# A long convolution with a routed expert layer: the matrices of the way back are turned on TensorE instead of loaded

## The chip, the cores and the metric

One core of a Trainium2 chip runs the whole program. The metric is the time of one execution in device microseconds (us). The engines are TensorE (PE in the rows, its weight loads PEld), VectorE (DVE), ScalarE (ACT), GpSimd (POOL) and SyncE (SP), which here only issues transfers. A row that ends in q (SPq, ACTq) is that engine's queue of instructions.

## The reference

Two layers follow each other. The first multiplies x and v (4 batches, 10048 positions, 128 channels), convolves the product over the positions with a filter that a small network makes, and multiplies by x again. The second sends every one of the 40192 rows to one of 16 experts and weighs what the expert gives.

```python
# first layer
h_filt = (np.maximum(pos_emb @ w1, 0.0) @ w2) * window
u = x * v
Uf = np.fft.rfft(u, n=2 * S, axis=1)
Hf = np.fft.rfft(h_filt, n=2 * S, axis=0)
y = np.fft.irfft(Uf * Hf[None, :, :], n=2 * S, axis=1)[:, :S, :]
x = (x * y).reshape(B * S, D)
# second layer: g = argmax(x @ w_group), e = argmax(x @ w_expert[g])
out = g_w * e_w * (np.maximum(x @ w1[g, e], 0.0) @ w2[g, e])
```

## The kernel before, in words

**The transform.** There is no FFT. A position is written as block times 128 plus place within the block, and the transform is done in two products with matrices of cosines and sines: one over the 79 blocks (`dft_blocks`, line 409), one over the 128 places within a block (`dft_positions`, line 487). Between them all of a batch lies in the tiles z and zr as frequency by channel: 128 places, 128 channels, 79 frequencies k, and two parts. All data are float32.

**Stages.** The filter goes first (up to about 143 us): its own transform ends in the DRAM array hspec. Then a loop runs over the batches b = 0 to 3 and once more for what is left of the last. For each batch:

- `dft_blocks` transforms the channels, three at a time, into z and zr. In the same loop the batch before comes out of z and zr: `turned` (lines 682 to 687) turns tiles through TensorE, ScalarE copies them to tiles tt, and `inverse_rest` and `inverse_blocks` (lines 697 and 718) make the second half of the inverse transform.
- Then 40 steps of `middle` and `back`, two frequencies each (the last has one). `middle` loads the filter's part ht (line 639). In every second step it loads four matrices bt from the constant c_b (line 644) and four matrices bp from the constant c_bp (line 645), one for each frequency: bt has the places on its partitions and the frequency's 128 outputs in its columns, and bp is the same matrix turned. `dft_positions` multiplies by bt into PSUM (tag ps, two buffers), VectorE multiplies by ht twice (lines 650 and 653), GpSimd adds and subtracts into y (lines 651 and 654). `back` is called LAG = 4 steps later: line 663 multiplies y by bp into PSUM (tag pt, four buffers), and ScalarE copies the result into z and zr (line 670), over what was read.
- While the steps of batch b run, the batch before it is routed, in pieces between the steps: `chosen` stores rows to DRAM (line 797), turns tiles of 128 by 128 through TensorE (line 800, copied by ScalarE at line 802), and multiplies them by the router's weights (lines 808, 817, 825). These turns, too, use PSUM's tag pt. `ranked` gives every row its place (VectorE, lines 854 to 894). Rows of batches ranked before are sent to the pages of their experts by GpSimd's indirect transfers (line 376), one in three steps of four.

Then the experts' pages are worked off (lines 1285 to 1376), from about 930 us on.

**What sets the order.** The transfers of lines 459 (input of the next batch), 639, 644, 645, 365 and 797 all stand in SP's queue. A transfer into a tile waits until the tile's buffer is free, and all behind it in the queue wait as well. bt shares five buffers (tag load) with the input xv; bp shares five (tag tt) with the turned tiles tt; ht shares five (tag spec) with the tiles xo. The order of each engine's instructions is fixed when the program is built, by a scheduler with a cost model that takes instructions by their place in the program as soon as it thinks them ready; some, such as the scatters, are held in the order in which the program names them. On the chip each engine takes its instructions in that order and stands where an operand is late.

A float32 matmul appears in the trace as two records of line 487 or 663; a turn as one.

Of the kernel before, what the change touches and what calls it, by code (L numbers as in the profile page):

```python
# [12 lines left out]
F32 = mybir.dt.float32  # L13
# [64 lines left out]
def make_consts():  # L78
    f32 = np.float32
    k1 = np.arange(NB)  # L80
    ang = 2 * np.pi * ((k1[None, :] * k1[:, None]) % N1) / N1
    w = (np.where(k1 == 0, 1.0, 2.0) / NN)[:, None]


    fa = np.stack(
        [
            np.stack([np.cos(ang), -np.sin(ang)], 2).reshape(NB, -1),
            np.stack([-np.sin(ang), -np.cos(ang)], 2).reshape(NB, -1),
        ],
        1,  # L90
    ).reshape(NB, -1)


    fi = []
    for swap in range(2):
        both = np.zeros((KM + 16, 2, NB))
        both[:NB, swap] = w * np.cos(ang)
        both[:NB, 1 - swap] = (2 * swap - 1) * w * np.sin(ang)
        rest = np.zeros((4, 32, 2, NB))
        for i in range(4):  # L100
            rest[i, :, i % 2] = both[KM:].reshape(32, NB)
        sign = 1 - 2 * swap
        fi += [sign * both[:KM].reshape(128, -1), sign * rest.reshape(128, -1)]
    fi = np.concatenate(fi, 1)
    k = k1[:, None] + N1 * np.arange(128)[None, :]
    s2 = 2 * np.arange(64) + 1
    a = np.pi * ((k[None] * s2[:, None, None]) % (2 * NN)) / NN
    b = np.concatenate([np.cos(a), np.sin(a)], 0)
    ph = (np.pi * ((k * 127) % (2 * NN)) / NN).T
    phase = np.stack([np.cos(ph), np.sin(ph), -np.cos(ph)], -1)  # L110
    win = np.zeros(NR * 128, f32)
    win[:SEQ] = np.exp(-0.01 * np.arange(SEQ, dtype=f32))
    win = win.reshape(NR, 128)
    return {
        "c_fa": np.concatenate([fa, np.zeros((NR - NB, 4 * NB))]),
        "c_fi": fi,
        "c_b": b,
        "c_bp": np.ascontiguousarray(b.transpose(2, 1, 0)),
        "c_phase": phase.reshape(128, NB * 3),
        "c_win": np.repeat(np.stack([win[:, 64:], win[:, 63::-1]]).transpose(0, 2, 1).reshape(2, -1), 64, 0),  # L120
        "c_tri": np.triu(np.ones((128, 128)), 1),
        "c_id": (np.arange(128)[:, None] * NB + np.arange(NB)[None, :]).astype(f32),
    }
# [26 lines left out]
class Kernel:  # L150
# [483 lines left out]
    def middle(self, b, k0, n):  # L634


        nc, d, sp = self.nc, self.d, self.sp
        ht = sp.tile([128, 2, 2, 128], F32, tag="spec", name="ht", bufs=NSPEC)
        nc.sync.dma_start(ht[:, :n], d["hspec"][:, k0 : k0 + n])
        if k0 % 4 == 0:  # L640
            self.bt = self.ap.tile([128, 4, 128], F32, tag="load", name="bt", bufs=NLOAD)
            self.bp = sp.tile([128, 4, 128], F32, tag="tt", name="bp", bufs=NTT)
            m = min(4, NB - k0)
            nc.sync.dma_start(self.bt[:, :m], d["c_b"][:, k0 : k0 + m])
            nc.sync.dma_start(self.bp[:, :m], d["c_bp"][:, k0 : k0 + m])
        bt, bp = self.bt[:, k0 % 4 :], self.bp[:, k0 % 4 :]
        ps = self.dft_positions(k0, n, bt)
        y = self.ap.tile([128, 2, 2, 128], F32, tag="y", name="y", bufs=NY)
        t0 = self.ap.tile([128, 2, 2, 128], F32, tag="prod", name="t0", bufs=NPROD)
        nc.vector.tensor_tensor(t0[:, :n], ps[:, :n], ht[:, :n], ALU.mult)  # L650
        nc.gpsimd.tensor_tensor(y[:, :n, 0], t0[:, :n, 0], t0[:, :n, 1], ALU.add)  # L651
        t1 = self.ap.tile([128, 2, 2, 128], F32, tag="prod", name="t1", bufs=NPROD)
        nc.vector.tensor_tensor(t1[:, :n], ps[:, :n], ht[:, :n, ::-1], ALU.mult)  # L653
        self.beyond(nc.gpsimd.tensor_tensor(y[:, :n, 1], t1[:, :n, 1], t1[:, :n, 0], ALU.subtract))  # L654
        return k0, n, bp, y
# [733 lines left out]
def build(nbat):  # L1389
    import concourse.bacc as bacc  # L1390

    nc = bacc.Bacc("TRN2", target_bir_lowering=False, num_devices=1, dynamic_dma_scratch_size=8192)
    shapes = {
        "xv_in": (nbat, NR, D, 2, 128),
        "x_out": (nbat, 128, D * NB),
        "pos_t": (128, 64 * NR),
        "p_w1": (128, 128),
        "p_w2": (128, 256),
        "w_router": (128, 32),
        "m_w1": (128, NE, FF),  # L1400
        "m_w2": (128, NE, FF),
        "c_iota": (128, 8 + NZ + 5 * NE),
    }
    for n, a in make_consts().items():
        shapes[n] = a.shape
    d = {n: nc.dram_tensor(n, s, F32, kind="ExternalInput").ap() for n, s in shapes.items()}
    d["out"] = nc.dram_tensor("out", (nbat * 128 * NB, D), F32, kind="ExternalOutput").ap()
    d["prow"] = nc.dram_tensor("prow", (Pages(nbat).rows, RW), F32, kind="Internal").ap()
    d["xyd"] = nc.dram_tensor("xyd", (nbat * 128 * NB, D), F32, kind="Internal").ap()
    d["hspec"] = nc.dram_tensor("hspec", (128, NB, 2, 128), F32, kind="Internal").ap()  # L1410
    with tile.TileContext(nc) as tc:
        Kernel(tc, d, nbat).emit()
    return nc


def layout(x, v, pos_emb, w1, w2, moe_w_group, moe_w_expert, moe_w1, moe_w2):
# [64 lines left out]
    for n, a in make_consts().items():  # L1481
        m[n] = c(a.astype(np.float32))
# [18 lines left out]
```

## Time and profile before

| | |
|---|---|
| median of three runs | 1888.68 us (1883.96 to 1894.56) |
| the profiled execution | 1889.78 us; span 1888.0 us |
| TensorE, weight loads | 1807.3 us (96%), 1522.5 us (81%) |
| VectorE, ScalarE, GpSimd | 1401.1, 1251.4, 1016.1 us (74%, 66%, 54%) |
| DMA | 343.81 MB, mean 182 GB/s |
| mean granted clock of TensorE | 0.989 of 2.4 GHz |

The profiled execution's own time holds some 1.8 us around the span, from the first to the last instruction. Busy time is the sum of an engine's instructions. Matmuls are pipelined: each has some 0.2 to 0.4 us from start to modelled end, and the next starts before that end, so the busy time of TensorE is not a measure of its room; the distance of two starts is. In the views used below, a line of the timeline merges neighbouring instructions of one kind (start, time from the first start to the last end, engine, line, tiles, count), and square brackets hold the idle time before it and what ended that. A wait for several things is put down to the one that came last.

### The profile page before, as it was taken

What the parts mean: (1) busy time and instruction counts of PE and PEld (TensorE: products, weight loads), DVE (VectorE), ACT (ScalarE), POOL (GpSimd) and SP (SyncE); (2) the same over time, 40 slices, a digit from 0 to 9 for tenths busy, and PEclk for the clock granted to TensorE, in tenths of its full rate; (3) what the DMA queues carried; (4) which work ended last, traced back from release to release, by engine and by line L of the source; (5) the groups of instructions that cost most, each with busy time, mean ns of one, the idle gap of its engine ahead of it and who ended that gap; (6) DMA issues with size and microseconds to landing.
All of it is one profiled execution on the core that took longest, in us unless ns stands there. A gap on an engine that the chain in (4) does not pass through costs nothing.

```text
span 1888.0 us, 43089 instructions
## 1 busy us (share of the span) xinstructions
PE 1807.3 (96%) x13958; PEld 1522.5 (81%) x13958; DVE 1401.1 (74%) x3140; ACT 1251.4 (66%) x2814; POOL 1016.1 (54%) x1172
## 2 busy tenths in 40 slices
PE   8988999999999999988899999999999999999998
PEld 7966888778877777767688888888888888889997
DVE  5577778689868975872879877777777777777886
ACT  6563368436743674456677777777777777777886
POOL 3236720464799478967245556666576333333354
PEclk9999999999999999999899999999999999999999
DMA  4599987987999799965563333444343223222342
GB/s 149 171 284 231 314 228 208 307 268 221 289 337 301 189 269 328 307 197 181 197 204 113 113 113 121 158 134 135 122 135 113 90 89 90 90 86 84 101 125 90
DMA packets 225451, 343.81 MB, mean 182 GB/s; under 512 B 28520, under 2 KB 110653, under 8 KB 225216
## 3 DMA queue, kind: packets, MB, share of 16 engines
q1 hardware_dynamic: 194208, 280.60, 49.3%
q0 software_dynamic: 21504, 44.82, 7.0%
q10 hardware_dynamic: 9504, 15.54, 3.0%
q8 instruction: 113, 1.85, 0.4%
q14 instruction: 122, 1.00, 0.2%
HBM read 265.88 MB, written 75.53 MB: 181 GB/s over the span
## 4 chain that ended last, share of the span: by engine, by line
PE 72%; DVE 9%; DMA 8%; issue 2%; ACT 2%; POOL 1%; SPq 1%; ACTq 0%; DVEq 0%; POOLq 0%
PE py L1352 8%; PE py L1350 8%; PE ph L1330 8%; PE ph L1332 8%; PE py L1351 8%; PE ph L1331 8%; PE psb L487 5%; PE pbp L663 4%; PE psa L409 3%; DMA xv<-xv_in 3%; PE po L718 2%; PE ptm L1364 2%; PE po L697 2%; PE px L1285 2%; DMA v<-xv_in 2%
## 5 line engine op out<-in xcount | busy, mean ns | idle before, releaser
L1339 DVE SCALAR_TENSOR_TENSOR hl<-ph,hh 128x512 fp32r<-128x512 f32 (+1 forms) x656 | 441.8, 674 | 157.5 <-ACT hh L1338 153.2
L1376 POOL DMA_INDIRECT out<-os,to x320 | 319.1, 997 | 416.4 <-ACT os L1371 344.0
L1338 ACT ACTIVATE hh<-ph 128x512 fp32r<-128x512 f32 (+1 forms) x656 | 388.7, 592 | 169.2 <-PE ph L1332 141.5
L376 POOL DMA_INDIRECT prow<-stg,adr x316 | 328.5, 1040 | 133.8 <-issue 61.8
L1330 PE MATMUL ph<-xh,wh 128*128 128x512 f32 (+2 forms) x720 | 280.9, 390 | 5.1 <-ACT wh L1312 5.1
L1332 PE MATMUL ph<-xh,wl 128*128 128x512 f32 (+2 forms) x720 | 265.8, 369 | 0.8 <-DVE ep L1247 0.8
L1331 PE MATMUL ph<-xl,wh 128*128 128x512 f32 (+2 forms) x720 | 264.7, 368 | 0.0
L1352 PE MATMUL py<-hh,wl 128*128 128x512 f32 (+2 forms) x720 | 264.6, 367 | 0.0
L1350 PE MATMUL py<-hh,wh 128*128 128x512 f32 (+2 forms) x720 | 264.5, 367 | 0.0
L1351 PE MATMUL py<-hl,wh 128*128 128x512 f32 (+2 forms) x720 | 263.3, 366 | 0.0
L670 ACT COPY z<-pbp 128x512 f32<-128x512 f32 x128 | 75.0, 586 | 179.3 <-PE pbp L663 173.8
L651 POOL TENSOR_TENSOR y<-t 128x256 f32<-128x256 f32 (+1 forms) x160 | 121.1, 757 | 132.0 <-DVE t L650 128.9
L409 PE MATMUL psa<-fa,eo 96*64 96x158 f32 x2048 | 171.4, 305 | 11.6 <-POOL eo L476 8.1
L487 PE MATMUL psb<-z,bt 128*128 128x256 f32 x640 | 162.7, 382 | 14.4 <-DVE t L653 5.8
L663 PE MATMUL pbp<-y,bp 128*128 128x256 f32 x632 | 162.8, 379 | 6.1 <-POOL y L654 4.2
L650 DVE TENSOR_TENSOR t<-psb,ht 128x512 f32<-128x512 f32 (+1 forms) x160 | 108.7, 679 | 73.6 <-POOL y L651 19.3
L409 PEld LDWEIGHTS psa<-fa,eo 96*64 96x64 f32 x2048 | 137.0, 139 | 28.2 <-POOL eo L476 12.7
L1332 PEld LDWEIGHTS ph<-xh,wl 128*128 128x128 f32 x720 | 136.7, 190 | 23.1 <-DVE ep L1247 1.1
L1330 PEld LDWEIGHTS ph<-xh,wh 128*128 128x128 f32 x720 | 137.2, 191 | 21.2 <-ACT wh L1312 5.6
L1351 PEld LDWEIGHTS py<-hl,wh 128*128 128x128 f32 x720 | 135.9, 189 | 21.9
L1352 PEld LDWEIGHTS py<-hh,wl 128*128 128x128 f32 x720 | 135.8, 189 | 21.9
L1350 PEld LDWEIGHTS py<-hh,wh 128*128 128x128 f32 x720 | 135.8, 189 | 21.3
(229 smaller groups left out, 3572.4 us busy)
## 6 DMA issues: line engine op xcount, KB each, us to landing
ws<-m_w SPq DMA_DIRECT2D x180, 256.0 KB
ht<-hspec SPq DMA_DIRECT2D x156, 256.0 KB
xv<-xv_in SPq DMA_DIRECT2D x131, 288.0 KB
bt<-c_b SPq DMA_DIRECT2D x95, 256.0 KB
bp<-c_bp SPq DMA_DIRECT2D x76, 256.0 KB
xyd<-xy SPq DMA_DIRECT2D x76, 256.0 KB
stg<-xyd SPq DMA_DIRECT2D x76, 256.0 KB
xg<-prow SPq DMA_DIRECT2D x66, 260.0 KB
```

Source lines behind the costliest of these rows:

```text
L376: ins = self.nc.gpsimd.indirect_dma_start(self.d["prow"], bass.IndirectOffsetOnAxis(ap=u.adr[:, t : t + 1], axis=0), u.rows[:, t - u.t0], ...
L409: ins = nc.tensor.matmul(ps[hs, i], eo[:, i, hs], self.fa[:, h], start=True, stop=True)
L487: nc.tensor.matmul(ps[:, i].rearrange("p s d -> p d s"), bt[:, i], self.frequency(k0 + i, 1)[:, :, 0], start=True, stop=True,)
L1330: k.fix(nc.tensor.matmul(ph[:, j], wh, self.xh, start=True, stop=False))
L1331: k.fix(nc.tensor.matmul(ph[:, j], wh, self.xl, start=False, stop=False))
L1332: k.fix(nc.tensor.matmul(ph[:, j], wl, self.xh, start=False, stop=True))
L1338: k.fix(nc.scalar.activation(hh, ph, AF.Relu))
L1339: k.fix(nc.vector.scalar_tensor_tensor(hl, ph, 0.0, hh.bitcast(F32), ALU.max, ALU.subtract))
L1350: k.fix(nc.tensor.matmul(self.py, wh, hh, start=(c == 0), stop=False))
L1351: k.fix(nc.tensor.matmul(self.py, wh, hl, start=False, stop=False))
L1352: k.fix(nc.tensor.matmul(self.py, wl, hh, start=False, stop=(c == NC - 1)))
L1376: ins = k.nc.gpsimd.indirect_dma_start(k.d["out"], bass.IndirectOffsetOnAxis(ap=self.to[:, h : h + 1], axis=0), o, None, bounds_check=k.nt ...
```

## The change

The constant c_bp and its load are gone. Where `middle` loads a group of bt, it takes a PSUM buffer of tag pt, turns each of the group's matrices (four, in the last group three) through TensorE against the identity, and lets ScalarE copy the whole group into bp. The tile bp stays where it was, with tag tt and five buffers.

```diff
@@ make_consts
         "c_b": b,
-        "c_bp": np.ascontiguousarray(b.transpose(2, 1, 0)),
         "c_phase": phase.reshape(128, NB * 3),
@@ middle
             self.bp = sp.tile([128, 4, 128], F32, tag="tt", name="bp", bufs=NTT)
             m = min(4, NB - k0)
             nc.sync.dma_start(self.bt[:, :m], d["c_b"][:, k0 : k0 + m])
-            nc.sync.dma_start(self.bp[:, :m], d["c_bp"][:, k0 : k0 + m])
+            pt = self.psT.tile([128, 4, 128], F32, tag="pt", name="ptb")
+            for i in range(m):
+                nc.tensor.transpose(pt[:, i], self.bt[:, i], self.ident)
+            nc.scalar.copy(self.bp[:, :m], pt[:, :m])
         bt, bp = self.bt[:, k0 % 4 :], self.bp[:, k0 % 4 :]
```

## Rows read from the trace of the kernel before

**Rows 1.** The chain that ended last, from the page of the whole execution.
```profile
PE 72%; DVE 9%; DMA 8%; issue 2%; ACT 2%; POOL 1%; SPq 1%; ACTq 0%; DVEq 0%; POOLq 0%
```

**Rows 2.** Instructions on tile bp: times (x) ns min/median/max, first and last start us.
```profile
L663 PE MATMUL pbp<-y,bp x632: 376/377/483, 182.8 to 822.8; 128*128 128x256 f32 x158
L645 SPq DMA_DIRECT2D bp<-c_bp x80: 327/382/1506, 171.7 to 803.3; - x80
```

**Rows 3.** Busy time of each engine in the windows M0, M1, M2 and M3.
```profile
core 0: us, PE busy (x) PEld busy (x) DVE busy (x) ACT busy (x) POOL busy (x), PEclk, DMA share, GB/s
...
179.20:252.00 72.80, 70.20 (x319) 59.00 (x320) 53.41 (x87) 23.02 (x41) 57.92 (x84) 1.00 0.91 288
...
336.00:432.50 96.50, 92.53 (x589) 71.65 (x585) 75.68 (x159) 40.78 (x96) 62.71 (x83) 1.00 0.87 285
...
521.00:624.00 103.00, 94.09 (x593) 71.37 (x589) 79.59 (x160) 40.87 (x97) 94.17 (x119) 1.00 0.91 302
...
721.00:823.50 102.50, 93.21 (x585) 71.42 (x579) 80.46 (x162) 40.55 (x95) 91.77 (x117) 1.00 0.84 282
```

**Rows 4.** Timeline of TensorE's weight loads, a step of M1 without routing.
```profile
410.66 0.84 PEld L487 LDWEIGHTS psb<-z,bt 128*128 128x128 f32 x4
411.53 0.83 PEld L663 LDWEIGHTS pbp<-y,bp 128*128 128x128 f32 x4
412.39 0.84 PEld L487 LDWEIGHTS psb<-zr,bt 128*128 128x128 f32 x4
```

**Rows 5.** Timeline of TensorE, a step of M1 with routing.
```profile
377.04 0.14 PEld L825 LDWEIGHTS pl<-ident,lt 128*128 128x128 f32 x1 [0.20 <-issue]
...
378.73 0.58 PEld L800 LDWEIGHTS ptr<-ident,xy 128*128 128x128 f32 x4
...
378.94 0.60 PE L800 MATMUL ptr<-ident,xy 128*128 128x128 f32 x4
...
379.83 0.14 PEld L825 LDWEIGHTS pl<-ident,lt 128*128 128x128 f32 x1 [0.20 <-ACT z L670]
```

**Rows 6.** Groups of instructions of the whole execution, shapes kept apart: busy us, mean ns.
```profile
L376 POOL DMA_INDIRECT prow<-stg,adr x316 | 328.5, 1040 | 133.8 <-issue 61.8 <-ACT zr L422 29.7 <-DMA xv<-xv_in 17.6
...
L651 POOL TENSOR_TENSOR y<-t 128x256 f32<-128x256 f32 x156 | 119.2, 764 | 131.9 <-DVE t L650 128.9 <-DVE c L870 0.8
...
L650 DVE TENSOR_TENSOR t<-psb,ht 128x512 f32<-128x512 f32 x156 | 107.1, 686 | 73.1 <-POOL y L651 19.3 <-POOL y L654 15.5 <-PE psb L487 13.2
...
L800 PE MATMUL ptr<-ident,xy 128*128 128x128 f32 x316 | 48.0, 277 | 4.0 <-DVE xy L735 4.0
...
L802 ACT COPY xrt<-ptr 128x512 f32<-128x512 f32 x76 | 44.3, 587 | 15.6 <-PE ptr L800 15.2
```

**Rows 7.** Timeline of TensorE's weight loads at the end of M2.
```profile
598.71 0.73 PEld L487 LDWEIGHTS psb<-zr,bt 128*128 128x128 f32 x4 [0.75 <-PE pbp L663]
...
605.84 0.73 PEld L487 LDWEIGHTS psb<-zr,bt 128*128 128x128 f32 x4 [1.05 <-PE pbp L663]
```

**Rows 8.** Waits of the whole execution: us in total, times, longest us.
```profile
DVE t L650 <- DMA ht<-hspec: 10.4, 5, 3.2
```

**Rows 9.** Timeline of M0: a load of bt, and TensorE's line 487 behind it.
```profile
184.76 0.38 SPq L644 DMA_DIRECT2D bt<-c_b  x1
...
189.01 1.97 PE L487 MATMUL psb<-z,bt 128*128 128x256 f32 x8 [0.40 <-DMA bt<-c_b]
...
199.69 1.11 PE L487 MATMUL psb<-z,bt 128*128 128x256 f32 x4 [1.03 <-DMA bt<-c_b]
```

**Rows 10.** Timeline of TensorE at the start of M1.
```profile
342.11 0.33 PE L825 MATMUL pl<-ident,lt 128*128 128x128 f32 x1
...
342.28 1.91 PE L487 MATMUL psb<-z,bt 128*128 128x256 f32 x8
...
347.28 1.11 PE L487 MATMUL psb<-z,bt 128*128 128x256 f32 x4 [0.75 <-DVE t L653]
```

## Prediction, made before the changed kernel was seen

> **What bounds the kernel now.** I read the page's chain first: TensorE fills 72% of the work that ended last, DMA 8% [rows 1]. That is an average over stages, so I asked which stages the change touches. The removed load is line 645's: 80 issues between 171.7 and 803.3 us [rows 2]. Cut by the first and last times of lines 487 and 663, there are four stretches of `middle` and `back`, one for each batch, called M0 to M3 here: 72.8, 96.5, 103.0 and 102.5 us, 374.8 in all [rows 3].
>
> In these stretches two rows of TensorE disagree. In M1 the matmuls are busy 92.53 of 96.50 us, the weight loads only 71.65 [rows 3]. The page says that ends of matmuls are modelled, so I went to starts. In a step of M1 without routing the four weight loads of line 487 start at 410.66, the four of line 663 at 411.53, and the next step's at 412.39: 1.73 us a step, each load beginning 0.03 us after the one before has ended [rows 4]. That is 1.73/8 = 0.216 us for each matmul. A batch has 158 records of line 663 (632/4, [rows 2]) and as many of line 487: 316 x 0.216 = 68.3 us, 94% of M0, where TensorE does nothing else. In M1 to M3 the routing of the batch before adds transposes and small matmuls: two such steps start their line 825 at 377.04 and 379.83, 2.79 us apart [rows 5]. The other engines need less for a step: two VectorE products of 0.69 us, two GpSimd sums of 0.76, a ScalarE copy of 0.59 or so [rows 6]. So TensorE sets the pace of M0, M1 and most of M2 and M3.
>
> The exception is the end of M2 and M3. From 598.71 to 605.84 us three steps of M2 take 2.38 us each, though TensorE still has 1.73 us of work; the weight loads wait 0.75 us before a step [rows 7]. GpSimd sets the pace there: two sums and, in three steps of four, a scatter of 1.04 us [rows 6] make 1.53 + 0.78 = 2.3 us.
>
> **The change, part by part.** Each time is of the profiled execution: span 1888.0, its own time 1889.78; the median of the runs is 1888.68, 1.1 less.
>
> *Removed: 80 loads*, some 20 MB, and 0.38 us of SP's queue for each [rows 2]. SP waits for buffers anyway, so the 0.38 us alone buy nothing. What the bytes can buy is what now ends in a wait on a transfer. VectorE waits 10.4 us for ht, five times [rows 8]. TensorE waits for bt twice, in M0: 0.40 us at 189.01, for a bt issued at 184.76, and 1.03 us at 199.69 [rows 9]. DMA is 0.91 busy there, at 288 GB/s [rows 3]; one bp less in front of each ht and bt brings these in. I take back the 1.4 us of M0 whole. Of the waits for ht, what reached TensorE at M1's start is 0.75 us [rows 10]; I take as much for M2 and M3, 2.3 us. Together 3.7; bounds: 0, and all 10.4 + 1.4 = 11.8.
>
> *Added on TensorE: 79 transposes for each batch, 316.* Nothing in the trace turns bt, but line 800 turns tiles of the same shape and type, 316 of them too: four take 0.60 us from the first start to the last end and one lasts 0.277, so the spacing is (0.60 - 0.277)/3 = 0.108 us [rows 5, 6]. The weight load behind the last turn is longer: from the start of line 825's turn at 342.11 to the next matmul of line 487 it is 0.17 us [rows 10]. A group of four is so 3 x 0.108 + 0.17 = 0.49 us, and 80 groups are 39.2. Bounds: 316 x 0.108 = 34.1 below, and above the weight loads of four turns, 0.58 us [rows 5], 46.4. I take 39.2, since its rows show the turns with the very neighbour that they will have.
>
> *What hides some of it.* At the end of M2 and M3 a step has 0.65 us to spare (2.38 - 1.73), a group of two steps 1.3, so 0.49 fits. Some five groups of each stretch lie there: 10 x 0.49 = 4.9 us. If GpSimd gets faster there, this cover is gone and they cost the same 4.9. At the starts of M1 to M3, before the first `back`, TensorE is not full; two groups each may fit: 6 x 0.49 = 2.9.
>
> *Added on ScalarE: 80 copies of 128x512, 0.587 us each* (line 802's, [rows 6]): 11.7 us a stretch, beside 23.02 to 40.87 us of work [rows 3]. The copied tile is needed by `back`, four steps (7 us) later. The copies stand in front of those of lines 670 and 802, for which PSUM's four buffers wait, which the turned tile shares. I cost them at nothing; ScalarE's idle half hides them. Bound above: each delays the pace by 0.1 us, 8 us in all; below nothing, since they replace no work of ScalarE.
>
> *Moved: the wait for bt.* The turns need bt before line 487 does, and TensorE's order is fixed when the program is built. Where they are put some steps ahead of the use, TensorE stands at them with `back` queued behind, and ScalarE's copy to z behind that. In M0 bt lands just in time [rows 9]. I take nothing, since the loads also come sooner; bounds: 0.5 us for each of M0's 20 groups, 10 us, and below the 1.4 us that are already counted.
>
> *Sum.* 39.2 - 4.9 - 2.9 - 3.7 = +27.7 us. What follows a stretch needs its z, so the delay goes straight through: 1889.78 + 27.7 = 1917.5 us, and from the median 1888.68 + 27.7 = **1916.4 us**, 1.5% slower.
>
> **The rivals.**
>
> *Covered.* The weight loads are busy 71.65 us of M1's 96.50 [rows 3]. Were the other 24.85 us free, 79 turns of 0.58/4 = 0.145 us (11.5 us) would fit in, and in every other stretch too (M0, the tightest, has 13.8 us left). For it: TensorE does wait at places in M2 and M3. Against: the starts of rows 4 follow at the matmuls' own rate, with 0.03 us between. The delay would be 0 to 9 us: 1889. Chance 0.10. The Trainium skill's page Perfetto Trace Analysis, section Identifying the Most-Contended Engine, holds that a matmul row's busy share looks worse than it is and that the share of weight loads is the good measure. By that measure a quarter of M1 is left and the sum would be +0; the starts of rows 4 leave almost nothing, and the trace decides.
>
> *Faster: the transfers set the pace.* DMA is 0.84 to 0.91 busy in the stretches [rows 3]. If the order of VectorE's and TensorE's work really follows late ht and bt, 20 MB less give back all 11.8 us of the named waits. It decides only where TensorE has the room for the turns as well, since their 39.2 us are more than that. For it: M0's late bt. Against: steps without any wait, as in rows 4. 1888.7 - 11.8 = 1877. Chance 0.06.
>
> *Dearer.* The turns run ahead of bt in M0 (+10), ScalarE's order holds PSUM (+8), and nothing is hidden or given back: 46.4 + 18 = 64 at most. Half of the extras on 39.2 make +48: 1937. For it: M0's margin. Against: ScalarE's idle half. Chance 0.10.
>
> That the change doesn't do what it says is hardly possible: the load and its array are gone.
>
> **How the numbers follow.** The forecast has 0.74, with a span of its own from 34.1 - 7.8 - 11.8 = +15 to 46.4 - 4.9 = +41: 1903 to 1930. To hold 8 in 10 the range takes in most of the dearer case and comes near the covered one: 1897 to 1936. About 0.5% (9.4 us) is what a measurement of this kernel can tell from no change. Slower by more than that: 0.74 + 0.10 = 0.84; within it: 0.10; faster: 0.06.
>
> **What would show it.** TensorE has 316 more matmuls against ident, 0.108 us apart within a group. M0 grows from 72.8 to about 81 us, M1 to about 104, M2 and M3 by some 5 to 6 each; a group of two steps in M1 is longer by 0.49. Waits for ht shrink, those for bt go, and DMA's share of M0 falls. Wrong would be: stretches that keep their length (covered) or shrink (transfers); a wait of the new turns on bt, or of line 663 on the new copy (dearer); or a change outside M0 to M3.

## The result, and the profile after

| | before | after |
|---|---|---|
| median of the runs side by side | 1889.38 us (4 runs) | 1904.18 us (4 runs, 1900.48 to 1905.1) |
| the same with runs of a later comparison | 1888.59 us (7 runs) | 1905.88 us (4 runs) |
| the profiled execution, its span | 1889.78, 1888.0 us | 1900.48, 1898.7 us |

The change makes the kernel slower: the ratio is 1.0085 with a 95% interval of 1.0065 to 1.0105, and 1.0095 (1.0069 to 1.0120) in the later comparison. That is 15 to 17 us, where 27.7 were forecast; 1904 us lies in the range of 1897 to 1936. The direction and the place were right, the size was not, and the experiments ask why.

In the changed kernel the turns are line 646 and ScalarE's copy is line 647; line 487 is now 486, 663 is 665, 670 is 672, 682 is 684, and 650 is 652. First, the chain of the page [rows 1]. Its shares reach only 57% of the span this time, so it is not comparable with the one of before, and I read the stages instead.

```profile
PE 52%; DVE 2%; ACT 2%; issue 1%; DMA 0%; POOL 0%; SPq 0%; ACTq 0%; DVEq 0%; POOLq 0%
```

The instructions on the turned tile, in the columns of [rows 2]: 316 turns are there, and 80 copies.

```profile
L646 PE MATMUL ptb<-ident,bt x316: 269/273/331, 177.1 to 828.9; 128*128 128x128 f32 x158
L647 ACT COPY bp<-ptb x80: 484/587/593, 177.8 to 829.3; 128x512 f32<-128x512 f32 x76, 128x384 f32<-128x384 f32 x4
```

Now the stages. From here on a stretch M0 to M3 is cut in every kernel in one way, from a batch's first matmul of `dft_positions` to the first turn of zr that follows (line 682 before); T1 to T4 are the times between, T4 up to the first page of the experts. Before, the stretches are so 72.4, 96.2, 102.8 and 102.5 us, 373.9 together. The turns of a batch's first group stand ahead of that cut, as here in M0, which begins at 177.62 (weight loads):

```profile
177.09 0.42 PEld L646 LDWEIGHTS ptb<-ident,bt 128*128 128x128 f32 x4 [0.22 <-issue]
177.62 1.60 PEld L486 LDWEIGHTS psb<-z,bt 128*128 128x128 f32 x8
```

So 76 of the 80 groups of turns lie inside the stretches, and four in what goes before them. The windows M0 to M3, then T3 and T4 of the kernel after (columns as in [rows 3]):

```profile
core 0: us, PE busy (x) PEld busy (x) DVE busy (x) ACT busy (x) POOL busy (x), PEclk, DMA share, GB/s
177.60:255.50 77.90, 77.21 (x393) 66.51 (x391) 54.44 (x89) 33.23 (x61) 58.59 (x84) 1.00 0.68 205
340.70:441.90 101.20, 99.96 (x655) 79.72 (x653) 76.27 (x160) 50.38 (x113) 62.61 (x83) 1.00 0.70 220
532.10:638.30 106.20, 100.57 (x654) 79.55 (x652) 81.57 (x160) 50.06 (x113) 91.33 (x118) 1.00 0.77 243
731.90:837.40 105.50, 100.33 (x655) 79.65 (x653) 81.03 (x164) 50.07 (x113) 90.73 (x117) 1.00 0.71 223
...
638.30:731.90 93.60, 89.17 (x1448) 78.96 (x1449) 76.13 (x206) 68.05 (x172) 56.25 (x62) 0.98 0.92 251
837.40:922.90 85.50, 76.49 (x1190) 61.13 (x1191) 40.66 (x130) 61.93 (x137) 46.31 (x49) 0.98 0.65 217
```

T3 and T4 of the kernel before:

```profile
624.30:721.20 96.90, 91.01 (x1445) 80.12 (x1445) 76.50 (x207) 67.90 (x171) 55.62 (x62) 0.97 0.93 242
823.70:912.00 88.30, 79.07 (x1189) 63.27 (x1190) 38.95 (x132) 62.18 (x137) 45.75 (x49) 0.94 0.65 210
```

| us | up to M0 | M0 | T1 | M1 | T2 | M2 | T3 | M3 | T4 | pages |
|---|---|---|---|---|---|---|---|---|---|---|
| before | 179.2 | 72.4 | 84.8 | 96.2 | 88.9 | 102.8 | 96.9 | 102.5 | 88.3 | 976.0 |
| after | 177.6 | 77.9 | 85.2 | 101.2 | 90.2 | 106.2 | 93.6 | 105.5 | 85.5 | 975.8 |
| difference | -1.6 | +5.5 | +0.4 | +5.0 | +1.3 | +3.4 | -3.3 | +3.0 | -2.8 | -0.2 |

So the four stretches give +16.9 us, and in these two executions the rest gives back 6.2. T1's +0.4 is the first group of M1: in all traces of this document T1 is 84.7 to 84.8 us where M1 begins without turns, 85.2 where it begins with one set, and 85.6 with two. In one group of later runs every kernel, the one before too, took 2075 to 2123 us, because the stages outside M0 to M3 were longer; from that group I compare stretches, and the ratio within it, alone. DMA's share in M0 falls from 0.91 to 0.68, and from 0.84-0.91 to 0.70-0.77 in the others. The steps are longer, as forecast: a steady group of M0 (weight loads, as in [rows 4], where two steps take 3.46 us) now takes 3.90, and the next matmul starts 0.43 us after the first turn.

```profile
189.72 0.57 PEld L646 LDWEIGHTS ptb<-ident,bt 128*128 128x128 f32 x4
...
193.62 0.57 PEld L646 LDWEIGHTS ptb<-ident,bt 128*128 128x128 f32 x4
...
197.53 0.57 PEld L646 LDWEIGHTS ptb<-ident,bt 128*128 128x128 f32 x4
```

The same group by its matmuls:

```profile
193.84 0.60 PE L646 MATMUL ptb<-ident,bt 128*128 128x128 f32 x4
194.27 1.03 PE L486 MATMUL psb<-z,bt 128*128 128x256 f32 x4
```

The wait of VectorE for ht, 10.4 us before [rows 8], is down to this (us, times, longest), and no wait for bt is left (ht's tag spec has four buffers, as line 60 says, and not five):

```profile
DVE t L652 <- DMA ht<-hspec: 3.2, 2, 1.6
```

### The profile page after: what moved, and what is told of

It reads as the page before. It is cut to its first block, busy times and chain, and to the rows that moved or that the text cites. A ratio compares the mean times of both kernels' runs of the same rounds, so it can differ in the third digit from the quotient of the medians.

```text
span 1898.7 us, 43704 instructions
## 1 busy us (share of the span) xinstructions
PE 1832.0 (96%) x14274; PEld 1551.3 (82%) x14274; DVE 1409.3 (74%) x3140; ACT 1291.1 (68%) x2894; POOL 1017.5 (54%) x1172
## 4 chain that ended last, share of the span: by engine, by line
PE 52%; DVE 2%; ACT 2%; issue 1%; DMA 0%; POOL 0%; SPq 0%; ACTq 0%; DVEq 0%; POOLq 0%
PE py L1354 8%; PE py L1352 8%; PE ph L1332 8%; PE ph L1334 8%; PE py L1353 8%; PE ph L1333 8%; PE ptm L1366 2%; PE px L1287 2%; PE po L699 1%; PE po L720 1%; PE ptr L802 0%; ACT oo L730 0%; PE plt L810 0%; ACT tt L689 0%; ACT oo L729 0%
## 5 line engine op out<-in xcount | busy, mean ns | idle before, releaser
L408 PEld LDWEIGHTS psa<-fa,eo 96*64 96x64 f32 x2048 | 134.3, 136 | 29.3 <-POOL eo L475 10.8
```

The source lines that it names most:

```text
L408: ins = nc.tensor.matmul(ps[hs, i], eo[:, i, hs], self.fa[:, h], start=True, stop=True)
```

## The experiments

All were read by the lengths of the stretches, and by time where there were several runs. Two theories stood against each other for what was missing in the stretches, 27.7 - 16.9 = 10.8 us. R: the loads that are gone gave back more than thought. F: the turns ran in more of the time in which TensorE waited anyway.

### Turns and loads

```diff
             m = min(4, NB - k0)
             nc.sync.dma_start(self.bt[:, :m], d["c_b"][:, k0 : k0 + m])
+            nc.sync.dma_start(self.bp[:, :m], d["c_bp"][:, k0 : k0 + m])
             pt = self.psT.tile([128, 4, 128], F32, tag="pt", name="ptb")
```

> The turns are kept and the 80 loads of bp come back; the turned copy then writes over what was loaded. Theory R (relief: the missing 20 MB gave back waits for ht and bt, at the start of M0 and in all four stretches): the stretches grow by 5 to 12 us beyond those of the changed kernel (77.9, 101.1, 106.2, 105.4 us), and the time is 1909 to 1917 us. Theory F (fill: the turns only went into time in which TensorE waited for VectorE and GpSimd anyway): the stretches stay within 2 us of those of the changed kernel and the time is 1902 to 1906 us.

> The kernel with turns and loads once more, beside the next two on the same chip, because the two chips so far differ outside the stretches. Its stretches are 395 to 398 us if the first trace was typical.

Measured: 1910.32 us (ratio to before 1.0107, 1.0084 to 1.0130). The stretches are 79.9, 101.3, 108.1 and 107.8 us, 397.1 together, and 397.1 again in the second trace, of which the windows M0 to M3 stand here:

```profile
175.20:254.80 79.60, 77.62 (x394) 66.54 (x392) 54.36 (x89) 33.36 (x61) 58.57 (x84) 1.00 0.84 267
340.00:441.30 101.30, 99.90 (x654) 79.65 (x652) 76.20 (x160) 50.18 (x113) 62.52 (x83) 1.00 0.83 269
534.20:642.50 108.30, 101.05 (x654) 79.67 (x652) 81.63 (x160) 50.08 (x113) 91.28 (x118) 1.00 0.87 287
738.10:846.00 107.90, 100.79 (x655) 79.75 (x653) 81.02 (x163) 50.03 (x113) 90.97 (x117) 1.00 0.81 267
```

Both theories have a part. The loads cost 5 to 6 us beside the turns (397.1 - 390.8 = 6.3, and 5.4 against the second trace of the changed kernel, 391.7), at the low end of what R asked. But the turns with the loads kept add only 397.1 - 373.9 = 23.2 us: some of their price is hidden, or it is lower than thought. One line of the second trace shows what the dearer rival had in mind (TensorE's weight loads in M0):

```profile
185.22 0.42 PEld L648 LDWEIGHTS ptb<-ident,bt 128*128 128x128 f32 x4 [1.51 <-ACT z L674]
```

Here the turns stand 1.51 us. The view of waits (us, times, longest) puts 1.1 us of the matmul's wait down to bt's transfer:

```profile
PE ptb L648 <- DMA bt<-c_b: 1.1, 1, 1.1
```

In the changed kernel this wait is not there.

### Turned twice

```diff
             for i in range(m):
                 nc.tensor.transpose(pt[:, i], self.bt[:, i], self.ident)
+                nc.tensor.transpose(pt[:, i], self.bt[:, i], self.ident)
```

> Each matrix is turned twice into the same place, so TensorE gets 316 more turns and nothing else changes. If a group of four costs TensorE 0.44 us wherever it stands, M0 and M1 grow by 8.7 us each against the changed kernel; if the ends of M2 and M3 still have room, those two grow by 6 to 8. Together 29 to 33 us: 1933 to 1937 us. If turns are hidden as the covered rival has it, the time stays under 1910 us.

Measured: 1941.47 us (1.0272, 1.0245 to 1.0299), above what was expected. The windows M0 to M3:

```profile
178.90:264.60 85.70, 85.18 (x469) 74.77 (x467) 54.39 (x89) 34.73 (x60) 58.61 (x84) 1.00 0.61 186
350.20:461.30 111.10, 107.87 (x729) 87.61 (x727) 80.38 (x166) 50.96 (x112) 59.58 (x83) 1.00 0.64 200
555.90:670.90 115.00, 108.00 (x729) 87.62 (x727) 85.21 (x169) 50.74 (x112) 89.93 (x117) 1.00 0.71 222
765.40:880.20 114.80, 108.02 (x730) 87.72 (x728) 84.99 (x175) 51.02 (x112) 89.32 (x117) 1.00 0.64 206
```

They are 426.6 us together, 35.8 more than with one turn, or 0.47 us for each of the 76 further groups. In sum nothing of it is hidden, at the ends of M2 and M3 neither (+8.8 and +9.3); M0 pays a little less (+7.8) and M1 more (+9.9) than 19 groups at the price that follows, 8.4. The steady group of M0 confirms it (weight loads of the first turn of two groups): 4.34 us, 0.44 more than with one turn.

```profile
200.54 0.14 PEld L646 LDWEIGHTS ptb<-ident,bt 128*128 128x128 f32 x1
...
204.88 0.14 PEld L646 LDWEIGHTS ptb<-ident,bt 128*128 128x128 f32 x1
```

So the price of a group is 0.44 us. All 80 groups are 35.2, the 76 inside the stretches 33.4, and the covered rival has fallen: a second set finds no room. The first set costs the stretches 23.2 us with the loads kept, so 10.2 of its 33.4 are hidden and the rest is paid: 8.4 for a stretch against +7.2, +5.1, +5.5 and +5.4 in the second trace with loads.

Where they are hidden is read from the starts of the steps. These are the ninth and the 27th step of M1 before, where M1 starts at 336.36:

```profile
354.22 1.03 PE L487 MATMUL psb<-z,bt 128*128 128x256 f32 x4
...
400.06 1.03 PE L487 MATMUL psb<-z,bt 128*128 128x256 f32 x4
```

and in the second trace with turns and loads, where M1 starts at 339.98:

```profile
358.02 1.03 PE L487 MATMUL psb<-z,bt 128*128 128x256 f32 x4
...
407.77 1.03 PE L487 MATMUL psb<-z,bt 128*128 128x256 f32 x4
```

Counted from M1's start, the ninth step is 0.2 us later with the turns, though four groups (1.76 us) stand in front of it; the 27th is 4.1 us later, so the nine groups between are paid in full; the end of M1 is 5.1 us later, though six more groups (2.6 us) have come. So 1.6 us are hidden at the start of M1 and 1.6 at its end. Counted in the same way, M2 and M3 hide 1.0 and 0.8 at their starts, 1.8 and 2.2 at their ends.

### Neither load nor turn

```diff
-            self.bp = sp.tile([128, 4, 128], F32, tag="tt", name="bp", bufs=NTT)
...
-            nc.sync.dma_start(self.bp[:, :m], d["c_bp"][:, k0 : k0 + m])
...
                 by_part[:, i],
-                bp[:, i],
+                self.ident,
                 y[:, i],
```

> The kernel before with neither load nor turn of bp: line 663's product takes the identity in its place, so the way back of the transform is left out, and the rows that are routed afterwards are other rows; only M0 to M3 and what comes before them are compared. Theory R: the start of M0 comes 1 to 2 us earlier, and the four stretches together are 6 to 12 us shorter than before (373.9 us by the same cut). Theory F: they are within 3 us of it.

Measured (windows M0 to M3; the time, 1901.46 us, has other rows on other pages and is not compared):

```profile
177.20:247.30 70.10, 68.96 (x317) 59.01 (x317) 54.50 (x89) 23.18 (x41) 58.53 (x84) 1.00 0.76 228
332.00:427.60 95.60, 92.19 (x579) 71.44 (x577) 75.32 (x159) 40.47 (x94) 62.70 (x83) 1.00 0.77 233
516.40:617.80 101.40, 93.35 (x578) 71.24 (x578) 81.61 (x159) 40.54 (x94) 93.20 (x118) 1.00 0.82 255
710.00:811.70 101.70, 93.34 (x580) 71.29 (x578) 81.46 (x162) 40.62 (x94) 92.96 (x117) 1.00 0.74 234
```

Together 368.8, 5.1 us less than before. That is under R's 6 and over F's 3: the loads cost the kernel before some 5 us, 2.3 of them in M0; DMA's share falls to 0.74-0.82. Seen from here, the turns without any load add 390.8 - 368.8 = 22.0 us, so 11.4 of their 33.4 are hidden, beside 10.2 with the loads. M0 starts at 177.2 instead of 179.2; but with turns and loads it started at 177.0 and 175.2, so that start is not the loads' doing.

### The two kernels once more

> The changed kernel once more, with a trace. If the half-speed pieces of TensorE's clock after the last stretch (two in the first trace, four before) fall by chance, their number or place differs here and the time of the stretch from M3's end to the first page moves with it by 1.7 us for each piece of 3.4 us; if the change itself brought fewer of them, there are two again. The time is 1900 to 1906 us.

> The kernel before once more, with a trace. The four stretches by the same cut are again 72.4, 96.2, 102.8 and 102.5 us within 1 us each; M0 starts at 179.2 us if that start is a property of the kernel, and within 176.5 to 179.5 if it varies by chance. The half-speed pieces of the clock fall at other places if they are chance. Time 1886 to 1895 us.

The changed kernel had 1905.88 us. Its stretches were 77.9, 101.1, 106.1 and 106.6 us: within 0.1 us of the first trace but for M3 (105.5 there). Both traces of this kernel caught the fastest execution of their group of four (1900.48 and 1901.0 us). T3 and T4:

```profile
641.00:732.10 91.10, 87.05 (x1448) 77.26 (x1449) 75.87 (x206) 67.98 (x172) 54.88 (x59) 1.00 0.93 257
838.70:923.40 84.70, 75.98 (x1189) 60.82 (x1190) 38.85 (x131) 61.87 (x137) 44.91 (x49) 0.98 0.67 219
```

So T3's granted clock is another one for the same kernel (0.98, then 1.00), and T4's the same.

The second trace of the kernel before is of the group with the longer stages. Its stretches were 72.9, 96.4, 100.6 and 101.1 us, so M2 and M3 missed the 1 us that was allowed: they began with less idle time (their ninth steps began after 17.0 and 16.9 us, 19.4 and 19.3 in the first trace). M0 started at 177.5: that start varies by chance, and the -1.6 of the table is none of the change's.

### What in the loads costs: bytes or the queue; and the copies

Small loads:

```diff
-            nc.sync.dma_start(self.bp[:, :m], d["c_bp"][:, k0 : k0 + m])
+            nc.sync.dma_start(self.bp[:, 0, :16], d["c_bp"][:, k0, :16])
             pt = self.psT.tile([128, 4, 128], F32, tag="pt", name="ptb")
```

> As the kernel with turns and loads, but each load of bp brings only 64 bytes for each partition (8 KB in place of 256): SP's 80 issues and their waits are there, the bytes are not. If the bytes made the difference between that kernel (397.1 us of stretches) and the changed one (390.7), the stretches are 389 to 392 us; if the place in SP's queue did, they are 396 to 398.

> 80 loads of 8 KB in place of 256, on the same chip. If bytes are what the loads cost, the stretches are 4 to 7 us shorter than those of turns_and_loads_2, M0 by 1.5 to 2 of them; if SP's queue is, within 1.5 us of them.

The first time the stretches were 391.6 us together, and beside the second run with full loads (397.1) 391.5. M0 and M3 of this one:

```profile
176.10:254.40 78.30, 77.51 (x393) 66.60 (x391) 54.33 (x89) 33.25 (x61) 58.62 (x84) 1.00 0.70 210
...
732.00:837.70 105.70, 100.30 (x654) 79.62 (x652) 81.06 (x163) 50.06 (x113) 90.62 (x117) 1.00 0.73 226
```

So it is the bytes: SP's 80 issues are all there, and 5.6 us are gone, as much as without any load (5.4 to 6.3). M0 has 1.3 of them, a little less than expected, M1 none, M2 and M3 2.1 and 2.2.

No copy by ScalarE (the loaded bp is used, nobody reads the turned tile):

```diff
             nc.sync.dma_start(self.bp[:, :m], d["c_bp"][:, k0 : k0 + m])
             pt = self.psT.tile([128, 4, 128], F32, tag="pt", name="ptb")
             for i in range(m):
                 nc.tensor.transpose(pt[:, i], self.bt[:, i], self.ident)
-            nc.scalar.copy(self.bp[:, :m], pt[:, :m])
```

> As the kernel with turns and loads, without ScalarE's copy of the turned tile: line 663's product uses the loaded bp, and the turned tiles are read by nobody. If the 80 copies cost nothing, the stretches are 395 to 399 us as with the copies (397.1); if the copies delay the pace by the 0.1 us that I gave as their bound, they are 388 to 391.

> Without ScalarE's copies, on the same chip as the run with them. If the copies cost nothing, the stretches are within 2 us of those of turns_and_loads_2; if each delays the pace by 0.1 us, they are 6 to 8 us shorter.

The first run, in the group with the longer stages, gave 392.4 us, between the two ranges, and decides nothing: the kernel before is 2.9 us shorter there too, by M2 and M3, and the kernel with loads and copies was not run in that group. The second, beside the run with the copies, gave 397.0 against 397.1. M0 and M1:

```profile
177.10:256.70 79.60, 77.63 (x394) 66.54 (x392) 54.38 (x89) 23.18 (x41) 58.58 (x84) 1.00 0.84 265
341.90:443.20 101.30, 99.88 (x655) 79.66 (x653) 76.19 (x160) 39.78 (x93) 62.51 (x83) 1.00 0.82 270
```

ScalarE is busy 10 us less in a stretch (23.18 against 33.36 in M0), and no stretch is shorter for it. The copies cost nothing that these two traces can show.

### Turns only where TensorE waits

```diff
-            nc.sync.dma_start(self.bp[:, :m], d["c_bp"][:, k0 : k0 + m])
+            if k0 < 8 or (b and k0 >= 60):
+                pt = self.psT.tile([128, 4, 128], F32, tag="pt", name="ptb")
+                for i in range(m):
+                    nc.tensor.transpose(pt[:, i], self.bt[:, i], self.ident)
+                nc.scalar.copy(self.bp[:, :m], pt[:, :m])
+            else:
+                nc.sync.dma_start(self.bp[:, :m], d["c_bp"][:, k0 : k0 + m])
```

> The kernel before, with turns for the first two groups of every batch and for the last five of batches 1 to 3, and loads for the rest. If turns at the starts and at the ends of M1 to M3 run in time in which TensorE waits anyway (theory F there), and the loads that are missing at the starts give ht and bt their place (theory R there), the stretches are 1 to 5 us shorter than before: 369 to 373 us, and the time is 1884 to 1889 us. If each turn costs its 0.44 us a group everywhere, the 23 groups add 10 us: 384 us and 1898 us.

The ratio to the kernel before, in this group, is 0.9983 (0.9960 to 1.0007): no difference that can be told. M0 to M3 are 70.1, 96.5, 101.5 and 103.6 us, 371.7 against 371.0 of before. So 23 groups of turns, 10 us at their price, are nearly all hidden or paid back, but the promised gain is in M0 alone. M3 lost 2.5 us against the kernel before, most of it ahead of its third step, where the router's turns wait 2.86 us for VectorE. The window of M0, and that of before in the same group:

```profile
176.80:246.90 70.10, 69.36 (x322) 59.49 (x321) 54.49 (x89) 24.35 (x43) 58.51 (x84) 1.00 0.90 294
```

```profile
177.50:250.40 72.90, 70.35 (x316) 58.52 (x316) 54.27 (x89) 23.18 (x41) 58.38 (x84) 1.00 0.90 290
```

The last run keeps the turns for the first two groups of M0 only (`if b == 0 and k0 < 8`).

> The kernel before, with turns for the first two groups of batch 0 alone and loads for the other 78. With more such turns M0 was 70.1 us in place of 72.4 to 72.9, so if those two loads are all that M0 lost to loads, M0 is 69.8 to 70.5 us here, M1 to M3 are as before (96.2, 100.6 to 102.8, 101.0 to 102.5) and the time is 2 to 3 us below the kernel before, which is at the edge of what can be measured. If M0's relief came with the other turns, M0 stays at 72 or more.

```profile
179.20:249.30 70.10, 69.38 (x322) 59.54 (x320) 53.66 (x88) 24.33 (x43) 58.03 (x84) 1.00 0.91 294
...
521.70:626.20 104.50, 94.85 (x578) 72.27 (x577) 79.38 (x159) 40.62 (x94) 92.37 (x118) 0.98 0.90 299
```

M0 is again 70.1 us, as without any load of bp: what M0 lost to loads it lost to the first two of them. But M2 was 104.5 us in this execution, 1.7 longer than in the first trace of before; TensorE's granted clock was 0.98 there and 1.00 in every other M2, and 0.02 of 104.5 us is 2.1, so I put this down to the clock and not to the change. The time is 1888.36 against 1887.76 us, ratio 1.0003 (0.9989 to 1.0018). A gain of 2.3 us in a stretch is not seen in the whole (the interval reaches to 2.1 us faster), and no version here beats the kernel before.

## Why the forecast was right in direction and too large

- **TensorE as the bound of the stretches**: right. Two steady steps went from 3.46 [rows 4] to 3.90 us, and a second set of turns was paid in full. The Trainium skill's page Perfetto Trace Analysis, section Identifying the Most-Contended Engine, takes the share of weight loads as a measure of TensorE's room; by it a quarter of M1 was left. The trace does not agree: in M0 and M1 after, the weight loads are busy 66.51 of 77.90 and 79.72 of 101.20 us, and yet the second set of turns made M0 7.8 and M1 9.9 us longer.
- **The price of the turns**, forecast 39.2: it is 35.2, and 33.4 inside the stretches, since four groups stand ahead of the cut. These 4.0 us are the largest miss of one term. The term that was mis-sized is the 0.17 us behind the last turn, taken from line 825 [rows 10]. In the steady groups a set of four costs 0.44, four times 0.11, so the weight load of the next matmul adds almost nothing. The lower bound, 34.1, was nearer.
- **What hides them**, forecast 7.8: 10.2, and 11.4 without the loads. M2 and M3 hid 2.9 and 3.0, where I had put 3.4 each; M0 hid 1.2, where I had put nothing. The miss is M1: I gave it no cover but at its start (1.0 us), since its steps without routing showed no wait [rows 4]; it hid 3.3, half of them at its end. There TensorE waited for GpSimd before; these are the last weight loads of M1 before:

```profile
426.82 0.30 PEld L487 LDWEIGHTS psb<-zr,bt 128*128 128x128 f32 x2 [0.40 <-issue]
427.15 1.70 PEld L663 LDWEIGHTS pbp<-y,bp 128*128 128x128 f32 x8
430.28 0.73 PEld L663 LDWEIGHTS pbp<-y,bp 128*128 128x128 f32 x4 [1.43 <-POOL y L654]
431.43 0.30 PEld L663 LDWEIGHTS pbp<-y,bp 128*128 128x128 f32 x2 [0.41 <-POOL y L654]
```

and after:

```profile
436.51 0.30 PEld L486 LDWEIGHTS psb<-zr,bt 128*128 128x128 f32 x2 [0.36 <-issue]
436.84 3.42 PEld L665 LDWEIGHTS pbp<-y,bp 128*128 128x128 f32 x16
440.70 0.30 PEld L665 LDWEIGHTS pbp<-y,bp 128*128 128x128 f32 x2 [0.44 <-POOL y L656]
```

  After, 16 of them run in a row. One reason is the order of TensorE's instructions, which the prediction took as it was. Behind the last matmul of `dft_positions` stand 18 records of `back` now and 14 before, as the rows show; in M1 to M3 it is 14 in every trace without turns in the last groups and 18 in every trace with them. So four records, 0.86 us of work at 0.216 each, have moved into a wait. The order is not all of it: in the run with turns at the starts and ends alone it is 18 too, and there the part of M1 from the 27th step on hid only 0.7 of 2.1 us. For the rest it can be said that TensorE is slower by the turns, so that VectorE and GpSimd are ahead of it when the stretch ends; that is argued and not shown. The cover at the ends of M2 and M3 was there, but not as a place for whole groups: the waits stay, and stand now behind the turns (weight loads at the end of M2, compare [rows 7]):

```profile
619.11 0.73 PEld L486 LDWEIGHTS psb<-zr,bt 128*128 128x128 f32 x4 [1.07 <-PE ptb L646]
...
624.97 0.73 PEld L486 LDWEIGHTS psb<-zr,bt 128*128 128x128 f32 x4 [0.72 <-PE ptb L646]
```

- **What the loads give back**, forecast 3.7: 5.1 without turns, 5.4 to 6.3 beside them. The mechanism was right (bytes in front of ht and bt, not SP's issues), M0's 1.4 was 1.7 to 2.3, the 0.75 for each of M2 and M3 was 0.8 to 2.4, and M1 got almost none (0.1 to 0.6).
- **ScalarE's copies at nothing**: borne out (397.0 us of stretches without them, 397.1 with them). **The turns' wait for bt at nothing**: right for the changed kernel, and only because the loads are gone; with them TensorE stood 1.51 us once in M0.
- **The sum for the stretches** is 33.4 - 10.2 - 6.3 = +16.9, where 27.7 was forecast. Of the 10.8 us between them 4.0 are the price, 1.8 the four groups ahead of the cut, 2.4 the cover and 2.6 the loads: all four fall on the same side, and so the forecast is too large by more than any one of them. The transfers' rival fell: DMA's share went from 0.91 to 0.68 in M0, and no stretch shrank.
- **Outside the stretches** I forecast nothing, and named a change there as a sign of being wrong; 4.4 us were given back in T1 to T4 of the profiled pair, more than all of it in T3 and T4. TensorE's granted clock was 0.97 and 0.94 there before, 0.98 and 0.98 after: less time at 1.2 GHz. T3's clock varies with one kernel, as its second trace shows. The medians are 15 to 17 us apart and the stretches 16.9 and 17.8 in the two traces of the changed kernel, so that not all of the 4.4 us is the change's; how much is, no run here settles.

## What to carry to other kernels

To see whether an engine has room for new work, take the distance between starts in a steady step, and multiply the new work to see if it is paid in full: doubling the turns told price and cover apart in one run. Cover can be larger than the waits in a steady step show: look at the start and the end of a stage, and expect the order of instructions to change there with the new work. Exchanging a load for work on the engine that sets the pace costs most of that work, however busy DMA looks, unless DMA's waits are on that engine's path.

## What was not expected of the hardware

- Turns of 128 by 128 in float32 follow each other at 0.11 us, and a matmul's weight load of 0.187 us behind the last of them hardly shows: the group costs 0.44 us.
- TensorE's clock in T4 was granted at 0.94 in both executions without turns in M3 whose T4 is comparable (88.3 us, and 88.4 with turns in M0 alone), and at 0.96 to 0.98 in the seven with turns there (84.7 to 86.3 us), all outside the group with the longer stages. But it was 0.96 in the run with neither load nor turn too (86.3 us, on other rows). Before T4 comes M3, where TensorE's matmuls are busy 93.02 of 102.50 us before and 100.33 of 105.50 after. Whether that keeps the clock up was not tried by itself.
